# The last stage of a decode block: its result in two PSUM banks, the last weight row in two column halves, and one load for w_up

## The chip, the cores and the metric

The kernel runs on one core of one Trainium2 chip. The metric is the device time in microseconds of one execution, given as the median of several runs. A profiled execution also has a span, from the first to the last instruction that the profiler recorded; the execution's time is a little longer than its span.

## What is computed

One token (`x`, 1024 numbers) goes through attention with a long key/value cache and then through a gated feed-forward block, both with a layer norm ahead and the input added behind. All inputs and the output are bfloat16.

```python
h  = x + softmax(q @ K^T * Dh**-0.5) @ V @ wo        # 32 query heads, 4 KV heads, 65536 keys, Dh = 128
n  = layernorm(h)
h2 = h + (gelu(n @ w_gate) * (n @ w_up)) @ w_down    # 1024 -> 3584 -> 1024
```

The caches hold 134 MB, and wq, wo, w_gate, w_up and w_down together 39 MB. Every byte of them is read once. The result is 1024 numbers.

## The kernel before, in words

**The stream.** All big inputs come through one ring of three slots in SBUF, 64 KB per partition each. `load` (L172) takes the next slot when its offset is 0, or an offset inside the present slot, and issues one DMA from SyncE. The order of the loads in the program is the order in which they are issued and queue up: wq, then the K and V caches in pieces of 8 MB, then wo (one load, L479), w_gate (one load, L535), w_up (two loads of four chunks each, L539 to L542) and w_down (five loads of 14, 7, 4, 2 and 1 rows, L560 and L579). A load is issued as soon as what lay at its place in the slot has been read.

**The weights of the last stages.** Each weight matrix has its contraction index spread over 128 partitions, and the rest of that index gives "chunks" or "rows": 32 for wo, 8 for w_gate and w_up, 28 for w_down. One row of w_down is 128 x 1024 bfloat16, 256 KB, of which each partition holds 2 KB. The vector to be multiplied is the stationary operand, padded to 32 columns with zeros (`padded`, L235), and the weights stream past it. A stationary operand of 32 columns fills a quarter of TensorE, so four matmuls with different column groups (`tile_position=(0, 32*g)`) can run beside each other; their results stand in partitions 0, 32, 64 and 96 (and the 31 below each hold what belongs to the zeros).

**TensorE's helper.** `mm` (L153) issues one matmul. With `loaded=True` the matmul is issued without a weight load of its own (L158), and uses what the one before it in the same column group loaded; the trace puts matmuls with a weight load at L156 and those without at L158. `keep` (L135) ties each TensorE instruction behind the one before it in the program, so TensorE's order is the program's.

**wo.** `row_mm` (L469) gives each row of wo to one column group, in two halves of 512 columns, the second with `loaded`. `evac` (L247) copies the two banks to `at_r`, one on VectorE, one on ScalarE.

**The residual.** `f_ps` (L486) is one PSUM bank tile of 128 x 256 float32. `out_mm` (L488) issues four matmuls of 256 columns, one for each column group g, which covers the output's columns 256g to 256g+255. L494 adds up `at_r` over partitions with a stationary operand of ones (float32, two passes for each matmul), L496 adds x. What stands in `f_ps` now is h. L498 turns it to columns for the second layer norm. `f_ps` is not emptied: the rows of w_down are added to it later.

**Gate and up.** `up_mm` (L528) issues seven matmuls of 512 columns for a chunk, 56 for a matrix, into two banks. `turned` (L507) copies the two banks to SBUF (VectorE and ScalarE) and transposes them with eight float32 transposes on TensorE. For w_gate VectorE and ScalarE then form the gelu; for w_up VectorE multiplies (L557) and writes `act_bf`, which L238 pads to `actz`, the stationary operand for w_down.

**w_down.** For each of the five loads, L583 issues one `out_mm` for each row: four weight loads and four matmuls of 256 columns. Behind `turned` and behind the first two loads `keep_busy` (L572) issues 8, 8 and 5 matmuls of 128 x 512 into a bank that nobody reads (`w_ps`).

**The end.** `seen_by_sync` (L565) makes SyncE wait for the last eight loads, for the last ScalarE copy and for GpSimd. L587 casts `f_ps` (97 partitions x 256) to `o_fin` in bfloat16 on VectorE, and L588 writes it out from partitions 0, 32, 64 and 96, four runs of 512 bytes.

Of the kernel before, what the change touches and what calls it, by code (L numbers as in the profile page):

```python
# [12 lines left out]
F32 = mybir.dt.float32  # L13
# [4 lines left out]
def kernel(  # L18
# [13 lines left out]
    nc = tc.nc  # L32
    P = 128
    D = A_x.shape[-1]
# [4 lines left out]
    F = B_w_gate.shape[1]  # L39
    DC = D // P  # L40
    FC = F // P
# [5 lines left out]
    CW = 16384  # L47
# [20 lines left out]
    ones_f = low.tile([P, P], F32, name="ones_f")  # L68
# [8 lines left out]
    x_row = lead.tile([P, D // 4], BF16, name="x_row")  # L77
    ident_bf = lead.tile([P, P], BF16, name="ident_bf")
# [5 lines left out]
    o_fin = lead.tile([P, D // 4], BF16, name="o_fin")  # L84
# [10 lines left out]
    ps_m = ctx.enter_context(tc.tile_pool(name="ps_m", bufs=1, space=PSUM))  # L95
# [48 lines left out]
    def pe(op):  # L144
        return keep(op, "pe")
# [7 lines left out]
    def mm(out, lhsT, rhs, start, stop, loaded=False, tile_position=None, skip_group_check=False):  # L153
        t = nc.tensor
        if not loaded:
            return pe(t.matmul(out, lhsT=lhsT, rhs=rhs, start=start, stop=stop, tile_position=tile_position,  # L156
                               skip_group_check=skip_group_check))
        op = t.add_instruction(mybir.InstMatmult(  # L158
            name=nc.get_next_instruction_name(), engine=t.engine, start_tensor_calc=start, stop_tensor_calc=stop,
            tile_size=(lhsT.shape[0], lhsT.shape[1]), tile_position=tile_position or (0, 0), ldweights=False,  # L160
            bass_skip_group_check=skip_group_check,
            ins=[t.lower_ap(rhs), t.lower_ap(lhsT, for_matmul_weights=True)], outs=[t.lower_ap(out, opt=True)]))
        reuses.add(op.ins.name)
        return pe(op)
# [5 lines left out]
    loads, pools, last = [], [], {}  # L170

    def load(src, off=0):  # L172
        n, w = src.shape[1], src.shape[2]
        if off == 0:
            slot[0] = (slot[0] + 1) % NSLOT
        assert off + n * w <= 2 * CW
        o = slot[0] * 2 * CW + off
        tv = ring[:, o:o + n * w].rearrange("p (n w) -> p n w", w=w)
        loads.append(nc.sync.dma_start(out=tv, in_=src).ins)
        return tv  # L180
# [20 lines left out]
    for bp in range(4):  # L201
        s0 = 64 * (bp // 2) + bp % 2
        nc.vector.tensor_copy(out=esel[:, bp, :, :],
                              in_=ident_bf[:, s0:s0 + 63:2].unsqueeze(1).to_broadcast([P, 4, 32]))
# [30 lines left out]
    def padded(i, vec, ncols, name):  # L235
        t = pt_tile(i, [P, ncols, 32], BF16, name)
        pools.append(nc.gpsimd.memset(t[:], 0.0))
        nc.vector.tensor_copy(out=t[:, :, 0], in_=vec)  # L238
        return t
# [171 lines left out]
    for n, u in enumerate(units):  # L411
        what, g, li = u
# [53 lines left out]
    def row_bank(name):  # L466
        return ps_w.tile([P, 512], F32, name=name, tag="w")
# [11 lines left out]
    wv = load(wo_v[:])  # L479
    for c in range(Hq):  # L480
        row_mm(at_ps, o2z[:, c, :], wv[:, c, :], c, c < 4, c + 4 >= Hq)
    at_r = low.tile([P, DS, 512], F32, name="at_r", tag="sc0")
    for s in range(DS):
        evac(at_r[:, s, :], at_ps[s][:], s)
    OW = D // 4
    f_ps = ps_f.tile([P, OW], F32, name="f_ps")  # L486

    def out_mm(stat, mov, first, last, groups=range(4)):  # L488
        for g in groups:
            mm(f_ps[32 * g:32 * g + 32, :], stat, mov(g), first, last, tile_position=(0, 32 * g),  # L490
               skip_group_check=True)
# [8 lines left out]
    layernorm_cols(h_t[:, :, 0], hn_bf[:], "ln2")  # L500
    hnz = padded(2, hn_bf[:], DC, "hnz")

    assert F <= CW and FC == 28
    GB = CW // F
    NF = FC // 4

    def turned(banks, name, tag):  # L507
        outs = []
        both = low.tile([P, 2, 512], F32, name=name + "_ev", tag=tag)
        for k in range(2):  # L510
            ng = min(4, NF - 4 * k)
            ev = both[:, k, :]
            last["act"] = evac(ev[0:32 * ng, :], banks[k][0:32 * ng, :], k)
            t_ps = ps_t.tile([P, 4, P], F32, name=name + "_t", tag="T")
            for b in range(4):
                tr(t_ps[:, b, 0:32 * ng], ev[0:32 * ng, b::4], ident_f[0:32 * ng, 0:32 * ng])
            outs.append((16 * k, 4 * ng, t_ps[:, :, 0:32 * ng:32]))
        return outs
# [5 lines left out]
    u_banks = [row_bank("wu_ps") for _ in range(2)]  # L524
    gv = B_w_gate.rearrange("(p c) n -> p c n", c=DC)
    uv = B_w_up.rearrange("(p c) n -> p c n", c=DC)

    def up_mm(banks, w, c, loaded):  # L528
        for s in range(NF):
            g = s % 4  # L530
            mm(banks[s // 4][32 * g:32 * g + 32, :], hnz[:, c, :],
               w.rearrange("p (m j) -> p m j", j=FC)[:, :, 4 * s:4 * s + 4],
               c == 0, c == DC - 1, loaded=(loaded or s >= 4), tile_position=(0, 32 * g))
# [2 lines left out]
    for c in range(DC):  # L536
        up_mm(g_banks, wg[:, c, :], c, False)
    g_t = turned(g_banks, "wg", "sc1")
    for c0 in range(0, DC, GB):  # L539
        wu = load(uv[:, c0:c0 + GB, :], c0 * F)  # L540
        for cc in range(GB):
            up_mm(u_banks, wu[:, cc, :], c0 + cc, False)  # L542
    g_ap = top.tile([P, FC], F32, name="g_ap")
    for j0, nj, src in g_t:
        nc.vector.tensor_copy(out=by_j(g_ap, j0, nj), in_=src)
# [11 lines left out]
        nc.vector.tensor_tensor(out=by_j(act_bf, j0, nj), in0=src, in1=by_j(gl, j0, nj), op=ALU.mult)  # L557

    wd_v = B_w_down.rearrange("(p c) n -> p c n", p=P)
    sizes = [14, 7, 4, 2, 1]  # L560
    assert sum(sizes) == FC
    actz = padded(3, act_bf[:], FC, "actz")
    w_ps = row_bank("w_ps")

    def seen_by_sync(ins):  # L565
        seen = nc.sync.nop()
        for i in ins:
            tc.add_manual_dep(seen.ins, i.name,
                              mybir.DependencyInfo(mybir.DependencyClass.Sync, mybir.DependencyReason.DATA),
                              reason="seen")  # L570

    def keep_busy(n, src):  # L572
        for _ in range(n):
            mm(w_ps[:], ident_bf[:], src, True, True)

    keep_busy(8, wu[:, 0, 0:512])
    busy = [8, 5, 0, 0, 0]
    c0 = 0
    for sz, nb in zip(sizes, busy):  # L579
        wv = load(wd_v[:, c0:c0 + sz, :], c0 * D)  # L580
        for cc in range(sz):
            c = c0 + cc
            out_mm(actz[:, c, :], lambda g: wv[:, cc, g * OW:(g + 1) * OW], False, c + 1 == FC)  # L583
        c0 += sz
        keep_busy(nb, wv[:, 0, 0:512])
    seen_by_sync(loads[-8:] + [last["act"].ins] + [x.ins for x in pools])
    nc.vector.tensor_copy(out=o_fin[0:97, :], in_=f_ps[0:97, :])  # L587
    nc.sync.dma_start(out=out[0, 0].rearrange("(g n) -> g n", n=OW), in_=o_fin[0:97:32, :])  # L588


# [28 lines left out]
```

## Time and profile before

| what | value |
|---|---|
| median of 3 runs | 408.0 us (407.77 to 408.11) |
| the profiled execution's own time | 407.74 us |
| its span | 405.9 us |
| mean granted TensorE clock | 0.899 |
| busy: TensorE, VectorE, ScalarE, GpSimd | 72%, 50%, 10%, 2% of the span |
| read from HBM | 173.02 MB, 426 GB/s over the span |

Between the profiled execution's time and its span lie 1.84 us that the profile doesn't cover. The page cuts the span into 40 equal slices and gives each engine's busy share in tenths. The chain of waits goes back from the last instruction: at each step to what released it, or to the instruction ahead of it on its engine. The timeline lists instructions in order of time, merged by kind: start, how long the merged group took, engine, line, operation, output and input, the count, and in brackets the idle time before it and what ended it. PE is TensorE's matmuls, PEld its weight loads, DVE VectorE, ACT ScalarE, POOL GpSimd, SP SyncE. A first matmul that waited for a DMA starts when that load has landed, so these starts tell when the pieces of the stream arrive.

### The profile page before, as it was taken

To read this page: it belongs to the slowest core of one execution; us is meant where nothing else is said; L and a number is where in the kernel's file an instruction comes from. 1 tells how busy PE (TensorE), PEld (TensorE's weight loads), DVE (VectorE), ACT (ScalarE), POOL (GpSimd) and SP (SyncE) were. 2 spreads that over 40 slices of the span, in tenths; PEclk is the share of its full clock that TensorE was granted. 3 is DMA by queue.
4 is the path that set the end of the run, shared out by engine and by line. 5 is a ranking of instruction groups with operands and counts; after the bars stand their busy time and mean duration, and the time that the engine had idled before them with its cause. 6 is when DMAs were issued, how large, how long until landed. Compare 5 with 4: busy or idle time off the path is not lost.

```text
span 405.9 us, 2664 instructions
## 1 busy us (share of the span) xinstructions
PE 294.3 (72%) x1500; PEld 64.2 (16%) x750; DVE 202.4 (50%) x185; ACT 40.9 (10%) x63; POOL 7.5 (2%) x17
## 2 busy tenths in 40 slices
PE   0170677758899695979969957997695999636285
PEld 0110111111111110221111113111110211212042
DVE  0200989999829744971595387609943000220110
ACT  1001000023000031100000312000031000100000
POOL 2000000000000000000000000000010000000000
PEclk9997689987899999769999967899999699886889
DMA  9999999999999999999999999999999999999995
GB/s 413 413 413 439 491 408 413 420 440 478 420 408 426 446 465 420 408 433 452 452 420 415 433 452 446 421 421 433 446 446 420 428 433 452 405 443 407 432 423 234
DMA packets 3773, 173.19 MB, mean 427 GB/s; under 512 B 425, under 2 KB 433, under 8 KB 689
## 3 DMA queue, kind: packets, MB, share of 16 engines
q1 hardware_dynamic: 3752, 173.02, 98.7%
q8 instruction: 9, 0.15, 0.1%
q14 instruction: 4, 0.02, 0.0%
q10 hardware_dynamic: 8, 0.00, 0.0%
HBM read 173.02 MB, written 0.00 MB: 426 GB/s over the span
## 4 chain that ended last, share of the span: by engine, by line
DMA 41%; PE 35%; DVE 21%; ACT 2%; issue 1%; SPq 0%; ACTq 0%; DVEq 0%
DMA ring<-in_A_k_cache_dram 30%; DVE ring L289 16%; PE acc_ps L158 16%; DMA ring<-in_B_w_down_dram 11%; PE qk_ps L156 6%; PE acc_ps L156 5%; PE qk_ps L158 5%; DVE mx L314 2%; ACT sc L310 2%; DVE pT L347 1%; PE o_ps L156 1%; PE at_ps L156 1%; DVE acc_sb L370 1%; PE at_ps L158 1%; PE nb_ps L156 0%
## 5 line engine op out<-in xcount | busy, mean ns | idle before, releaser
L289 DVE STREAM_TRANSPOSE ring<-ring 128x2048 uint32<-128x2048 uint32 x64 | 142.7, 2279 | 35.5 <-DMA ring<-in_A_k_cache_dram 35.5
L156 PE MATMUL qk_ps<-ring,wsel 128*128 128x512 bf16 x256 | 107.2, 419 | 49.1 <-DVE ring L289 30.0
L158 PE MATMUL qk_ps<-ring,wsel 128*128 128x512 bf16 x256 | 106.4, 416 | 0.0
L158 PE MATMUL acc_ps<-ring,pT 128*128 128x512 bf16 x384 | 105.1, 383 | 0.0
L156 PEld LDWEIGHTS <-wsel 128*128 128x128 bf16 x256 | 27.0, 105 | 156.0 <-issue 139.1
L156 PE MATMUL acc_ps<-ring,pT 128*128 128x512 bf16 x128 | 49.2, 384 | 0.0
L314 DVE TENSOR_REDUCE mx<-qk_ps 128x1 f32<-128x1024 f32 x16 | 19.5, 1220 | 24.6 <-ACT sc L310 18.6
L347 DVE STREAM_TRANSPOSE pT<-pT 128x1024 bf16<-128x1024 bf16 x16 | 19.3, 1227 | 23.8 <-ACT pT L341 23.8
L156 PEld LDWEIGHTS <-pT 128*128 128x128 bf16 x128 | 12.8, 100 | 90.7 <-issue 90.7
L310 ACT COPY sc<-qk_ps 128x1024 f32<-128x1024 f32 x12 | 12.1, 1012 | 148.2 <-PE qk_ps L158 148.2
L370 DVE COPY acc_sb<-acc_ps 32x512 f32<-32x512 f32 x8 | 5.3, 666 | 29.4 <-PE acc_ps L158 29.4
L341 ACT ACTIVATE pT<-sc,nbias 128x1024 bf16<-128x1024 f32 x12 | 13.7, 1142 | 44.9 <-DVE nbias L333 41.9
L156 PE MATMUL ln_tot<-ln_s,ones_f 128*128 128x1 f32 x8 | 1.9, 311 | 13.4 <-DVE ln_s L210 11.6
L156 PE MATMUL q_ps<-ring,xnz 128*32 128x512 bf16 x32 | 5.0, 598 | 9.1 <-DMA ring<-in_A_wq_dram 9.1
L156 PE MATMUL o_ps<-sel,acc_sb 128*128 128x8 f32 x32 | 6.6, 335 | 5.8 <-DVE rl L384 5.4
L372 ACT COPY acc_sb<-acc_ps 32x512 f32<-32x512 f32 x8 | 4.6, 577 | 58.6 <-DVE acc_sb L370 58.6
L156 PE MATMUL wu_ps<-ring,hnz 128*32 128x512 bf16 x32 | 4.7, 502 | 7.7 <-DMA ring<-in_B_w_up_dram 7.7
L156 PE MATMUL wg_ps<-ring,hnz 128*32 128x512 bf16 x32 | 4.8, 539 | 7.1 <-DMA ring<-in_B_w_gate_dram 7.1
L248 DVE COPY q_ev<-q_ps 128x512 f32<-128x512 f32 x1 | 0.7, 692 | 14.0 <-PE q_ps L158 14.0
L341 ACT ACTIVATE pT<-qk_ps,nbias 128x1024 bf16<-128x1024 f32 x4 | 4.5, 1113 | 29.8 <-PE acc_ps L158 16.8
L156 PEld LDWEIGHTS o_ps<-sel,acc_sb 128*128 128x128 f32 x32 | 6.3, 293 | 6.1 <-issue 5.1
L156 PEld LDWEIGHTS <-hnz 128*32 128x32 bf16 x64 | 3.2, 115 | 20.8 <-issue 17.3
(105 smaller groups left out, 89.1 us busy)
## 6 DMA issues: line engine op xcount, KB each, us to landing
ring<-in_B_w_gate_dram SPq DMA_DIRECT2D x1, 7168.0 KB
ring<-in_B_w_up_dram SPq DMA_DIRECT2D x2, 3584.0 KB, 37.6
ring<-in_B_w_down_dram SPq DMA_DIRECT2D x1, 3584.0 KB, 38.2
ring<-in_B_w_down_dram SPq DMA_DIRECT2D x1, 1792.0 KB, 41.6
ring<-in_B_w_down_dram SPq DMA_DIRECT2D x1, 1024.0 KB, 43.3
ring<-in_B_w_down_dram SPq DMA_DIRECT2D x1, 512.0 KB
ring<-in_B_w_down_dram SPq DMA_DIRECT2D x1, 256.0 KB, 44.2
ring<-in_A_k_cache_dram SPq DMA_DIRECT2D x8, 39.4
```

The lines of the kernel that those rows point to most:

```text
L156: return pe(t.matmul(out, lhsT=lhsT, rhs=rhs, start=start, stop=stop, tile_position=tile_position, skip_group_check=skip_group_check))
L158: op = t.add_instruction(mybir.InstMatmult(name=nc.get_next_instruction_name(), engine=t.engine, start_tensor_calc=start, stop_tensor_calc ...
L248: return nc.vector.tensor_copy(out=dst, in_=src) if k % 2 == 0 else nc.scalar.copy(out=dst, in_=src)
L289: dv(nc.vector.transpose(out=kt[:, c * w:(c + 1) * w], in_=kt[:, c * w:(c + 1) * w]))
L310: ac(nc.scalar.copy(out=sc[:], in_=flat))
L314: dv(nc.vector.tensor_reduce(out=state[("mx", g)][:, li:li + 1], in_=flat, axis=AX.X, op=ALU.max))
L341: ac(nc.scalar.activation(out=flat, in_=state.pop(("sc", g, li)), func=ACT.Exp, bias=st["nbias"][:, 0:1], scale=scale, accum_out=st["lpart ...
L347: dv(nc.vector.transpose(out=flat, in_=flat))
L370: dv(nc.vector.tensor_copy(out=acc_sb[sl, :], in_=acc[sl, c, :]))
L372: ac(nc.scalar.copy(out=acc_sb[sl, :], in_=acc[sl, c, :]))
```

## The change

- w_up comes in one load, and its 56 matmuls follow that load.
- The result of the last stage stands in two PSUM banks: `f_ps[:, 0:128]` for the output's columns 0 to 511, and a new tile `fb_ps` of 128 x 128 for columns 512 to 1023. In each, column group g covers 128 columns. `half_mm` issues one matmul of 128 columns.
- h is formed a second time, in this layout, by eight float32 matmuls over `at_r` and eight with x; they stand behind the transposes of w_up in TensorE's order. The first h, in `f_ps`, still feeds the layer norm.
- w_down comes in loads of 16, 8 and 3 rows, and the 28th row in two loads of 512 columns. A row of the first 27 is four weight loads and eight matmuls of 128 columns; the second of each two reuses the weights. A half of the last row is four weight loads and four matmuls.
- `keep_busy` issues 4 matmuls behind the seeds of h, 10 behind the 16 rows and 3 behind the 8 rows.
- The first half is cast by VectorE, the second by ScalarE, each 97 x 128, and one DMA writes both: eight runs of 256 bytes.

```diff
-    assert F <= CW and FC == 28
-    GB = CW // F
+    assert DC * F <= 2 * CW and FC == 28
...
-    for c0 in range(0, DC, GB):
-        wu = load(uv[:, c0:c0 + GB, :], c0 * F)
-        for cc in range(GB):
-            up_mm(u_banks, wu[:, cc, :], c0 + cc, False)
+    wu = load(uv[:])
+    for c in range(DC):
+        up_mm(u_banks, wu[:, c, :], c, False)
...
-    sizes = [14, 7, 4, 2, 1]
-    assert sum(sizes) == FC
...
-    keep_busy(8, wu[:, 0, 0:512])
-    busy = [8, 5, 0, 0, 0]
+    HW = D // 2
+    QW = HW // 4
+    fb_ps = ps_m.tile([P, QW], F32, name="fb_ps", tag="misc")
+    halves = [f_ps[:, 0:QW], fb_ps[:]]
+
+    def half_mm(b, g, stat, mov, first, last, loaded=False):
+        mm(halves[b][32 * g:32 * g + 32, :], stat, mov, first, last, loaded=loaded, tile_position=(0, 32 * g),
+           skip_group_check=True)
+
+    for g in range(4):
+        for b in range(2):
+            half_mm(b, g, ones_f[:, 0:32], at_r[:, b, g * QW:(g + 1) * QW], True, False)
+    for g in range(4):
+        for b in range(2):
+            q = 2 * b + g // 2
+            half_mm(b, g, ident_bf[:, 32 * q:32 * q + 32], x_row[:, g % 2 * QW:(g % 2 + 1) * QW], False, False)
+
+    def down_rows(wv, c0, n, bs):
+        for cc in range(n):
+            c = c0 + cc
+            for g in range(4):
+                for b in bs:
+                    o = (b if len(bs) > 1 else 0) * HW + g * QW
+                    half_mm(b, g, actz[:, c, :], wv[:, cc, o:o + QW], False, c + 1 == FC, loaded=(b > bs[0]))
+
+    keep_busy(4, wu[:, 0, 0:512])
     c0 = 0
-    for sz, nb in zip(sizes, busy):
+    for sz, nb in zip([16, 8, 3], [10, 3, 0]):
         wv = load(wd_v[:, c0:c0 + sz, :], c0 * D)
-        for cc in range(sz):
-            c = c0 + cc
-            out_mm(actz[:, c, :], lambda g: wv[:, cc, g * OW:(g + 1) * OW], False, c + 1 == FC)
+        down_rows(wv, c0, sz, [0, 1])
         c0 += sz
         keep_busy(nb, wv[:, 0, 0:512])
-    seen_by_sync(loads[-8:] + [last["act"].ins] + [x.ins for x in pools])
-    nc.vector.tensor_copy(out=o_fin[0:97, :], in_=f_ps[0:97, :])
-    nc.sync.dma_start(out=out[0, 0].rearrange("(g n) -> g n", n=OW), in_=o_fin[0:97:32, :])
+    assert c0 == FC - 1
+    o_b = o_fin[:].rearrange("p (b j) -> p b j", b=2)
+    for b, put in ((0, nc.vector.tensor_copy), (1, nc.scalar.copy)):
+        wv = load(wd_v[:, c0:FC, b * HW:(b + 1) * HW], c0 * D + b * HW)
+        down_rows(wv, c0, 1, [b])
+        if b == 1:
+            seen_by_sync(loads[-8:] + [last["act"].ins] + [x.ins for x in pools])
+        put(out=o_b[0:97, b, :], in_=halves[b][0:97, :])
+    nc.sync.dma_start(out=out[0, 0].rearrange("(b g n) -> g b n", b=2, g=4),
+                      in_=o_b[0:97:32, :, :])
```

## Prediction, made before the result was known

> **What bounds the kernel now.** First the page: its head, the slices, the chain.
>
> ```profile
> span 405.9 us, 2664 instructions
> ...
> DMA  9999999999999999999999999999999999999995
> ...
> HBM read 173.02 MB, written 0.00 MB: 426 GB/s over the span
> ...
> DMA 41%; PE 35%; DVE 21%; ACT 2%; issue 1%; SPq 0%; ACTq 0%; DVEq 0%
> ```
>
> The DMA engines are full in 39 of 40 slices, and no byte is read twice. So the time is the stream's length, about 402.65 us, and a tail behind its last byte. The chain of waits over the last 36 us shows the tail:
>
> ```profile
> 358.49 44.16 DMA ring<-in_B_w_down_dram
> 402.65 0.04 issue
> 402.69 0.32 PE f_ps L156 x4
> 403.00 0.02 issue
> 403.03 0.42 DVE o_fin L587
> ```
>
> Behind the last w_down row come one row of matmuls, the cast and the write. Last the timeline, where each f_ps group starts when a load has landed, and SyncE's write closes the work:
>
> ```profile
> 394.10 1.71 PE L156 MATMUL f_ps<-ring,actz 128*32 128x256 bf16 x56 [1.58 <-DMA ring<-in_B_w_down_dram]
> ...
> 398.42 0.95 PE L156 MATMUL f_ps<-ring,actz 128*32 128x256 bf16 x28 [0.77 <-DMA ring<-in_B_w_down_dram]
> ...
> 400.86 0.62 PE L156 MATMUL f_ps<-ring,actz 128*32 128x256 bf16 x16 [0.31 <-DMA ring<-in_B_w_down_dram]
> ...
> 402.06 0.40 PE L156 MATMUL f_ps<-ring,actz 128*32 128x256 bf16 x8 [0.58 <-DMA ring<-in_B_w_down_dram]
> ...
> 402.69 0.29 PE L156 MATMUL f_ps<-ring,actz 128*32 128x256 bf16 x4 [0.23 <-DMA ring<-in_B_w_down_dram]
> ...
> 403.48 0.64 SPq L588 DMA_DIRECT2D out_dram<-o_fin  x1
> ```
>
> TensorE waits for all five loads, so the stream and not TensorE sets 402.69. From there the tail is 0.34 to the cast, 0.45 to the write, 2.42 from the write to the span's end. About 0.2% of the time, 0.8 us, is what a measurement here can tell from no change, and the edit can shorten only the first two terms, 0.79 us together.
>
> **The stream, part by part.** Landings go by those starts: 7 rows in 4.32 us, 4 in 2.44, 2 in 1.20, 1 in 0.63, so 0.61 to 0.63 us a row. The new pieces should land at 394.10 + 2 x 0.617 = 395.33 (16 rows), 400.86 - 0.61 = 400.25 (24), 402.06 (27), about 402.37 (first half), 402.69 (second). Shorter runs could cost: the single row took 0.02 us more than its share of the two rows ahead (0.63 against 0.60, rounding and all), so two halves may cost 0 to 0.05. One load less for w_up could save as much. I take zero for both.
>
> w_up's single load needs its whole slot free. Its second half was issued at 347.19 (SyncE's queue in the timeline), 21 us ahead of w_gate's landing at 368.72; one load issued then still queues behind w_gate. The w_down loads stand behind it on SyncE, issued from 355.88; they need wo's rows read (done by 357.6), which doesn't move. Nothing stalls; cover 21 us.
>
> **TensorE before w_down.** All 56 w_up matmuls now wait for 385.62. w_gate is the row for that: one load, 56 matmuls from 368.72, VectorE's copy of the first bank at 374.08, 5.36 later, half of it at the low clock (the stage 385.6 to 389.3 had a granted clock of 0.50 too). So the copy for w_up starts at 390.98 instead of 388.84, 2.14 us late, and all up to `actz` with it: ready at 391.30 + 2.14 = 393.44, while TensorE leaves the transposes at 390.85 + 2.14 = 392.99. The seeds of h have as many columns as L494 and L496 had, which took 358.45 to 359.19 at the low clock: 0.37 to 0.74 us. Four `keep_busy` matmuls at 0.215 (seven recorded took 1.67, one 0.379) are 0.86. TensorE is free at 394.3 to 394.6; the 16 rows land at 395.33. Cover 0.7 us: price nothing.
>
> **TensorE in w_down.** A row of 256-column matmuls costs 0.109 us now: 56 starts span 1.71 - 0.27 over 13 row steps. A row becomes eight matmuls of 128 columns, as many columns, with four weight loads as before. That pairs in one column group don't block the other groups is shown by wo, where each group got two matmuls in a row, the second at L158: four of 512 columns went every 0.215 us (starts at 355.67, 355.89, 356.10). By columns a new row costs 0.11. But issuing may bind: the shortest matmuls of the trace tell.
>
> ```profile
> 351.82 0.25 PE L156 MATMUL o_ps<-o_sb,osel 32*128 32x32 bf16 x4 [0.30 <-DVE o_sb L455]
> ```
>
> Each takes 171 ns by its row, so starts are (0.25 - 0.171)/3 = 26 ns apart, where a quarter of a 128-column matmul's columns flow. Eight at 26 would be 0.21 us a row. These four were in no column groups, so the price lies between 0.11 and 0.21; I take 0.11, the row with the same tiling.
>
> With r for a row: 16 r from 395.33, ten `keep_busy` 2.46 (2.15, and 0.3 for the change of tiling ahead of them; today 0.16 passes from the end of the 14 rows' record at 395.81 to the next start at 395.97), 8 r, three 0.85, 3 r and the halves r. By r = 0.11, the 16 rows and ten matmuls end at 399.6, before 400.25; 8 rows and three end at 402.0, just before 402.06; 3 rows at 402.4; the halves meet their landings. If TensorE never waits again, it starts the last matmul at 395.33 + 2.46 + 0.85 + 28 r - 0.03 = 398.61 + 28 r, past 402.69 once r exceeds 0.146; from 400.25 the second stretch gives a like bound, 0.135.
>
> The Trainium skill ("TensorE: Matmul & The Clock Gate", on the 56 ns gap) says that start-to-start never falls below about 25 ns however short the matmul; the 26 ns agree. It speaks against the edit, which halves matmuls: by it a row is 0.20 and the forecast about 409.3. "TensorEngine Tiling (Array Packing)", Key Properties, says that tiles operate independently; if the floor holds for each tile alone, a row stays 0.11. No row here has short matmuls in column groups.
>
> **The tail.** The last piece is one half: four 128-column matmuls. Their record interpolates between 171 ns (32 columns) and 273 (256) to 215, 0.06 less, so the second copy starts 0.28 after the landing. The copy is ScalarE's:
>
> ```profile
> L270 ACT CAST wsel<-qr_ps 32x128 bf16<-32x128 f32 x4 | 1.0, 256 | 1.8 <-PE qr_ps L156 1.7
> ```
>
> That is the same form, 128 float32 of PSUM to bfloat16, and takes 0.256 against the 0.424 of VectorE's cast, 0.17 less. VectorE's half is beside it: landed 402.37, matmuls to 402.65, cast 0.29 (from 0.424 at 256 columns and 0.692 at 512), done 402.94, while ScalarE ends at 403.23. ScalarE's queue holds nothing else then. Sum: 0.06 + 0.17 = 0.23 off the tail; SyncE writes at 403.26. SyncE also waits for one engine more; its waits pass while the copies run. The write has eight runs of 256 bytes for four of 512. Below nothing I see no reason; above, x's load, four runs too, kept its queue 1.08 us against 0.64 here, so +0.44 for the issue, and if the 1.0 us that SyncE waits for the landing doubled, +1.0. The five w_down loads have 128 runs each and took 3.04 us of issuing, 0.61 apiece, no more than the four runs: I take 0.
>
> "DMA: Bandwidth & Descriptors", Specifications, calls 512 bytes the least for line rate, and says smaller ones are read, modified and written. It gives no price for eight of them, and no run here shows one.
>
> **The sum.** 405.9 - 0.23 = 405.7 in span; with the 1.84 outside it, 407.5 for the profiled execution, which had 407.74. That one lay 0.26 under the median of 408.0, so the forecast is 408.0 - 0.2 = 407.8, a gain too small to tell.
>
> **Rivals.**
> - *A tie or a little slower, 408.3 (18%).* TensorE takes 13.7 ns for each instruction, as today (eight in 0.109 us): twelve make r = 0.164, the last start 403.20, 0.51 late, less 0.23: +0.3. Or the write costs more, up to +1.0 - 0.2. For it: more instructions for the same columns. Against: those eight are explained by columns alone.
> - *TensorE becomes the bound, 409.5 (13%).* r = 0.21 puts the last start at 404.5, 1.8 late; less 0.23 is +1.5. It decides from r = 0.154, where 0.23 of lateness eats the gain. For it: the 26 ns. Against: wo's four groups side by side.
> - *The clock is late, 407.8 to 408.3.* If w_up ran wholly at the low clock, `actz` would come some 1.5 us later and the waits of 0.65 us ahead of the 8 rows and the 0.7 ahead of the 16 take most of it up. It is counted in the other cases.
> - *The change doesn't shorten the tail, 408.0:* the cast wasn't last, or the second bank brings nothing. The chain shows the cast on the path, so this is within the first case.
>
> **How the numbers follow.** 62% for the forecast (shortest matmul record 171, w_up's load saving 0.05, and the runs' own spread of 0.2 reach down to 407.4; upward to 408.0), 18% for the tie, up to 408.8, 13% for TensorE, 3% for something else slower, 4% for a gain over 0.8 us that I can't derive. Range 407.4 to 408.8 holds 80%. Faster by over 0.2% 0.04, within 0.80, slower 0.16.
>
> **What would show it.** f_ps and fb_ps groups starting at about 395.3, 400.25, 402.1, 402.4 and 402.7 with "DMA w_down" as the end of their idle time; 27 rows at 0.11 us; ScalarE's cast near 0.26, starting 0.28 after the last landing; SyncE's write near 403.26 and 2.4 us from it to the end. It is wrong if the last groups have no idle time ahead of them (TensorE bound), if the last landing moves from 402.7, or if the write takes longer.

## The result and the profile after

The changed kernel takes 408.82 us (median of 14 runs, 408.61 to 409.06), the kernel before 408.0 (14 runs, 407.7 to 408.39): 1.0021 times as long (1.0014 to 1.0028). The forecast was 407.8, so the sign was wrong, and the time lies just past the range. The page of the changed kernel:

```profile
span 406.9 us, 2822 instructions
...
PE 294.8 (72%) x1634; PEld 64.1 (16%) x774; DVE 202.1 (50%) x185; ACT 41.2 (10%) x64; POOL 7.5 (2%) x17
...
q8 instruction: 9, 0.15, 0.1%
...
HBM read 173.02 MB, written 0.00 MB: 425 GB/s over the span
```

The same lines of the page of the kernel before:

```profile
PE 294.3 (72%) x1500; PEld 64.2 (16%) x750; DVE 202.4 (50%) x185; ACT 40.9 (10%) x63; POOL 7.5 (2%) x17
...
q8 instruction: 9, 0.15, 0.1%
```

The bytes are the same, the span is 1.0 us longer. TensorE has 1634 + 774 = 2408 recorded instructions, before it had 1500 + 750 = 2250. The lines of q8 will matter below. The timeline of the changed kernel's last 12 us, cut to each first group behind a landing, the last group of the 16 rows (397.37) and the tail:

```profile
395.64 0.24 PE L156 MATMUL f_ps<-ring,actz 128*32 128x128 bf16 x4 [1.16 <-DMA ring<-in_B_w_down_dram]
...
397.37 0.25 PE L158 MATMUL fb_ps<-ring,actz 128*32 128x128 bf16 x4
...
400.48 0.24 PE L156 MATMUL f_ps<-ring,actz 128*32 128x128 bf16 x4 [0.60 <-DMA ring<-in_B_w_down_dram]
...
403.21 0.24 PE L156 MATMUL f_ps<-ring,actz 128*32 128x128 bf16 x4 [0.90 <-DMA ring<-in_B_w_down_dram]
...
403.81 0.24 PE L156 MATMUL fb_ps<-ring,actz 128*32 128x128 bf16 x4
...
403.83 0.29 DVE L611 CAST o_fin<-f_ps 97x128 bf16<-97x128 f32 x1 [10.52 <-PE f_ps L156]
404.10 0.27 ACT L611 CAST o_fin<-fb_ps 97x128 bf16<-97x128 f32 x1 [12.45 <-PE fb_ps L156]
404.39 0.68 SPq L612 DMA_DIRECT2D out_dram<-o_fin  x1
```

TensorE is never late: at the landings of 16, 24 and 27 rows it had been idle for 0.6 to 1.2 us, and the last half's matmuls (403.81) start 0.27 behind the first half's, where the step from group to group is 0.06. The tail did what it should: from the last half's first matmul (403.81) to the write (404.39) pass 0.58 us, where there were 0.79. The write to the end takes 406.9 - 404.39 = 2.51 instead of 2.42. But the loads are late. 16 rows came at 395.64 and 24 at 400.48, 0.2 to 0.3 behind the forecast; the three rows came at 403.21 instead of 402.06, and the last half at 403.81, 1.12 behind the last row of before. The sum, 1.12 - 0.21 + 0.09 = 1.00, is the span's difference.

At the 24 rows the landing is 0.23 behind the forecast, at the 27 rows 1.15: most of the loss arises in the stream's last three microseconds. The DMA view from 402 to 404 us, in slices of 0.05 us, first before and then after (each packet is counted where it starts):

```profile
GB/s 164 164 246 41 451 41 0 0 0 0 0 0 0 0 0 0 0 0 0 0 0 0 0 0 0 0 0 0 0 0 0 0 0 0 0 0 0 0 0 0
```

```profile
GB/s 184 144 123 123 225 102 41 21 41 143 20 0 0 0 41 20 20 20 20 41 21 20 20 20 20 20 41 0 0 0 0 0 0 0 0 0 0 0 0 0
```

Before, the last weights start by 402.3 and are in by 402.38. After, most is in by 402.55, and then something trickles at 20 to 41 GB/s until 403.35. Sixteen engines together move 426, some 27 each: this is about what one engine moves, about 1 us behind the others. The same view from 396 to 402 us has, besides the stream's queue q1, before and after:

```profile
q1 hardware_dynamic: 451, 2.23, 89.2%
```

```profile
q1 hardware_dynamic: 445, 2.17, 87.5%
q8 instruction: 1, 0.02, 1.0%
```

One packet of a queue that the page calls "instruction" is in that stretch after, and none before. By the trace's packets it has 16 KB and lasts from 400.36 to 401.30. Both kernels have nine of them. Before, the ninth starts at 402.243, six thousandths of a microsecond behind a completion packet of the stream at 402.237 (behind the data of each load the trace has 16 packets of 4 bytes; they are called completion packets here).

**Theories.** *R, refill:* these packets bring TensorE's instructions, 16 KB at a time, over the DMA engines that carry the stream. Each costs the DMA engine that carries it more than a microsecond. The change gives TensorE more instructions, so the ninth comes 2 us earlier and in front of weights instead of behind them. *S, size of runs:* the loads of 6 KB, 1 KB and 1 KB runs are slow. *U:* the one load of w_up makes the stream late.

### The profile page after: what moved, and what is told of

The parts are those of the page before. It is cut to its first block, busy times and chain, and to the rows that moved or that the text cites. A ratio compares the mean times of both kernels' runs of the same rounds, so it can differ in the third digit from the quotient of the medians.

```text
span 406.9 us, 2822 instructions
## 1 busy us (share of the span) xinstructions
PE 294.8 (72%) x1634; PEld 64.1 (16%) x774; DVE 202.1 (50%) x185; ACT 41.2 (10%) x64; POOL 7.5 (2%) x17
## 4 chain that ended last, share of the span: by engine, by line
DMA 40%; PE 38%; DVE 17%; ACT 2%; issue 1%; ACTq 0%; DVEq 0%
DMA ring<-in_A_k_cache_dram 30%; PE acc_ps L158 16%; DVE ring L289 12%; DMA ring<-in_B_w_down_dram 11%; PE qk_ps L156 8%; PE qk_ps L158 7%; PE acc_ps L156 5%; DVE mx L314 2%; ACT sc L310 2%; DVE pT L347 1%; PE o_ps L156 1%; DVE acc_sb L370 1%; PE at_ps L156 1%; PE at_ps L158 1%; ACT acc_sb L372 1%
## 5 line engine op out<-in xcount | busy, mean ns | idle before, releaser
L156 PE MATMUL qk_ps<-ring,wsel 128*128 128x512 bf16 x256 | 108.8, 425 | 49.4 <-DVE ring L289 30.2
L158 PE MATMUL qk_ps<-ring,wsel 128*128 128x512 bf16 x256 | 108.3, 423 | 0.0
```

The source lines that it names most:

```text
L158: op = t.add_instruction(mybir.InstMatmult(name=nc.get_next_instruction_name(), engine=t.engine, start_tensor_calc=start, stop_tensor_calc ...
```

## The experiments

Each time is a median; the kernel before ran beside each (medians 407.92 to 407.96).

**1. Before, with 48 tiny matmuls ahead.** Only TensorE's instruction count changes.

```diff
+    fill_ps = ps_m.tile([P, 32], F32, name="fill_ps", tag="misc")
+    for _ in range(48):
+        mm(fill_ps[:], ident_bf[:], ident_bf[:, 0:32], True, True)
     assert D // 4 == 32 * DC
```

> Theory R (refill): TensorE's instructions come in pieces of 16 KB over the DMA engines that carry the stream; each costs the engine that brings it some 1.4 us; before needs eight inside the stream and the ninth starts at 402.24, behind its engine's last weight, while the changed kernel, with more TensorE instructions, gets the ninth at 400.36, in front of weights. By R the kernel before with 48 tiny matmuls (96 instructions with their weight loads) ahead of everything, in time that TensorE waits for w_q, becomes slower by 1.0 to 1.4 us: 409.0 to 409.4. Theory S (size of runs): the shorter runs of the last loads make the stream late. By S this kernel, whose loads are those of before, stays at 408.0.

Measured: 409.02 (6 runs, 408.85 to 409.54), ratio 1.0027 (1.0015 to 1.0039). Its timeline, where the 48 matmuls stand at the start, and the last two loads:

```profile
1.51 1.46 PE L156 MATMUL fill_ps<-ident_bf 128*128 128x32 bf16 x48 [1.51 <-POOL ident_bf masks.py:199]
```

```profile
403.34 0.40 PE L156 MATMUL f_ps<-ring,actz 128*32 128x256 bf16 x8 [0.62 <-DMA ring<-in_B_w_down_dram]
403.93 0.29 PE L156 MATMUL f_ps<-ring,actz 128*32 128x256 bf16 x4 [0.19 <-DMA ring<-in_B_w_down_dram]
```

1.46 us of work in the first 3 us, while TensorE waits for wq anyway, make the last row land 1.24 us later (403.93 for 402.69), with loads that are those of before. All nine q8 packets moved, from 55.3, 115.8, 164.0 ... 390.1, 402.2 to 28.6, 96.0, 144.4 ... 374.0, 398.4: they follow TensorE's instructions. This is R; by S and by U nothing would have moved.

**2. The changed kernel with fewer TensorE instructions.** Rows of wo and chunks of w_gate and w_up are left out.

```diff
-    for c in range(Hq):
-        row_mm(at_ps, o2z[:, c, :], wv[:, c, :], c, c < 4, c + 4 >= Hq)
+    for c in range(8):
+        row_mm(at_ps, o2z[:, c, :], wv[:, c, :], c, c < 4, c + 4 >= 8)
...
-    for c in range(DC):
+    for c in (0, DC - 1):
         up_mm(g_banks, wg[:, c, :], c, False)
...
-    for c in range(DC):
+    for c in (0, DC - 1):
         up_mm(u_banks, wu[:, c, :], c, False)
```

> The changed kernel with fewer TensorE instructions: 24 of wo's 32 rows, six of w_gate's eight and six of w_up's eight chunks are loaded but left out of the sums (the output is not the reference's). Its loads are those of the changed kernel. By R the ninth refill falls behind the stream, the last half lands near 402.7 and the time is 407.6 to 407.9, faster than before by the 0.2 us of the tail. By S it stays at 408.8.

Measured: 408.33, but spread from 407.69 to 409.43 (10 runs). It doesn't decide. A stage of the profiled execution, which took 409.35 (start and end, length, then busy time of each engine, then the granted clock, here 0.50), shows why for that execution:

```profile
394.00:399.00 5.00, 3.43 (x128) 2.84 (x63) 0.00 (x0) 0.00 (x0) 0.00 (x0) 0.50 0.92 395
```

In this stage the clock was 0.50; ten `keep_busy` matmuls took 3.20 us, the eight rows waited for them until 402.24, and the casts began at 404.64. What fell was the cover that the forecast had counted on, by a cause of the experiment's own. Three of the ten runs, at 407.69 to 407.86, are where R put them. The profiled execution's weights were all in by 402.52, although a refill, here the eighth, stood in the stream at 400.26, almost where the changed kernel's ninth did: a refill in front of the last weights doesn't cost by itself (the last section comes back to this).

**3. Before, with w_up in one load.**

```diff
-    for c0 in range(0, DC, GB):
-        wu = load(uv[:, c0:c0 + GB, :], c0 * F)
-        for cc in range(GB):
-            up_mm(u_banks, wu[:, cc, :], c0 + cc, False)
+    wu = load(uv[:])
+    for c in range(DC):
+        up_mm(u_banks, wu[:, c, :], c, False)
```

> The kernel before with w_up in one load, and nothing else of the change. TensorE's instructions are as many as before. By R: 408.0, within 0.2. A third theory, U (one load of w_up makes the stream or actz late, since w_up's matmuls started 0.35 us later in the changed kernel's trace), gives 408.3 to 408.8.

Measured: 407.97 (10 runs), ratio 1.0 (0.9991 to 1.0009). U falls. Its w_up landed at 386.00, as late as in the changed kernel (385.98, before 385.62); over all runs here that first start lies between 385.5 and 386.5, so the 0.3 us there is not the change's. What sets it was not tried.

**4. The changed kernel with its last row in one load.**

```diff
+    wv = load(wd_v[:, c0:FC, :], c0 * D)
+    down_rows(wv, c0, 1, [0, 1])
     for b, put in ((0, nc.vector.tensor_copy), (1, nc.scalar.copy)):
-        wv = load(wd_v[:, c0:FC, b * HW:(b + 1) * HW], c0 * D + b * HW)
-        down_rows(wv, c0, 1, [b])
```

> The changed kernel with its 28th row in one load of 2 KB runs, then both halves' matmuls and both casts side by side. TensorE's instructions differ from the changed kernel's by four. By R the refill still falls into the stream: 408.8 to 409.0. By S, if the 1 KB runs are what is slow, it falls back to 408.0 to 408.2.

Measured: 409.03 (6 runs), ratio 1.0028 (1.0015 to 1.0041). The timeline still has the three rows late, and the ninth refill is at 400.06:

```profile
403.09 0.24 PE L156 MATMUL f_ps<-ring,actz 128*32 128x128 bf16 x4 [1.16 <-DMA ring<-in_B_w_down_dram]
```

The 1 KB runs are not what is slow. The 6 KB runs of the three rows were not undone by themselves; run 8 below keeps them and has them on time.

**5. The first 16 rows folded.** A kernel with the same result, the changed kernel's loads, casts and write, and TensorE instructions as few as before (1536 + 712 = 2248).

```diff
-    c0 = 0
-    for sz, nb in zip([16, 8, 3], [10, 3, 0]):
+    dn_ps = [row_bank("dn_ps") for _ in range(2)]
+    wv = load(wd_v[:, 0:16, :])
+    for c in range(16):
+        row_mm(dn_ps, actz[:, c, :], wv[:, c, :], c, c < 4, c + 4 >= 16)
+    s_r = low.tile([P, 2, 512], F32, name="s_r", tag="sc1")
+    for b in range(2):
+        nc.vector.tensor_tensor(out=s_r[:, b, :], in0=dn_ps[b][:], in1=at_r[:, b, :], op=ALU.add)
+    keep_busy(10, wv[:, 0, 0:512])
+    for b in range(2):
+        for g in range(4):
+            half_mm(b, g, ones_f[:, 0:32], s_r[:, b, g * QW:(g + 1) * QW], False, False)
+    c0 = 16
+    for sz, nb in zip([8, 3], [3, 0]):
```

The seeds over `at_r` go, those with x open the banks, and in `keep_busy` all but the first matmul of a burst get `loaded=True`.

> The changed kernel with fewer TensorE instructions and the same result: the first 16 rows go the way of wo's rows (each row to one column group, one weight load and two matmuls of 512 columns, three instructions instead of twelve), VectorE adds their two banks to at_r, and the ones matmuls fold the sum into the two halves; keep_busy loads its weights once a burst. Loads, casts and write are the changed kernel's. By R the ninth refill falls behind the stream as in the kernel before, and what is left is the shorter tail: 407.6 to 407.9, 0.2 faster than before. By S 408.8 stays.

Measured: 407.98 (11 runs, 407.55 to 409.32), ratio 1.0001 (0.9992 to 1.001). In the profiled execution the refill is gone from the stream (403.7); 0.8 of the loss is gone from the median, but the gain isn't there. Two stages of the profiled execution, the slowest of the runs:

```profile
393.40:395.90 2.50, 0.81 (x3) 0.09 (x1) 0.18 (x1) 0.00 (x0) 0.00 (x0) 1.00 0.96 413
395.90:399.30 3.40, 3.36 (x32) 0.67 (x15) 0.00 (x0) 0.00 (x0) 0.00 (x0) 0.50 1.02 434
```

TensorE worked 0.81 of 2.5 us, and the clock fell to 0.50 for the next 3.4: the 32 matmuls took all of them, and the last half waited for TensorE. That is one execution; the others' clocks in this stage aren't known.

**6. Fewer instructions again, w_up whole.** As in 2, without the third edit.

> The run with fewer instructions again, now with w_up whole: only 24 of wo's rows and six of w_gate's chunks are left out of the sums (the output is not the reference's). In the last one the clock was low in the w_down stage and TensorE late; with w_up's 56 matmuls in place the clock should be full from w_up on. By R: no refill between 393 and 402, last half at 402.7 to 402.9, 407.6 to 407.9. By S: 408.8.

Measured: 407.73, eight of ten runs from 407.49 to 407.81, the two others 408.52 and 409.04; ratio 0.9998 (0.9989 to 1.0007). Where the changed kernel's fourteen runs never came below 408.61, the same loads with fewer TensorE instructions come to 407.7. S falls. The profiled execution is the one of 408.52; its stream lost 0.7 us long before, around 60 to 77 us, where runs of 64 KB took 2.55 us for 2.42, so its late landings tell nothing of the change. The expectation "no refill between 393 and 402" was wrong: the eighth came at 399.70, on an engine that was ahead (below).

**7. Before, with 8 tiny matmuls.** As in 1, with `range(8)`.

> The kernel before with 8 tiny matmuls (16 instructions) ahead instead of 48. By R the ninth refill is asked for 16 instructions earlier; how near the kernel before stands to the edge isn't known: if the 16 bring it in front of some of the last weights, 408.3 to 409.2, if not 408.0. By S 408.0.

Measured: four runs at 408.00 to 408.06 and four at 409.09 to 409.87; ratio of all 1.0018 (1.0006 to 1.003). The profiled execution is one of the longer four, and its timeline shows the edge:

```profile
402.08 0.40 PE L156 MATMUL f_ps<-ring,actz 128*32 128x256 bf16 x8 [0.60 <-DMA ring<-in_B_w_down_dram]
...
404.21 0.29 PE L156 MATMUL f_ps<-ring,actz 128*32 128x256 bf16 x4 [1.73 <-DMA ring<-in_B_w_down_dram]
```

All weights are in by 402.38, as before. But the refill starts at 402.169, in front of one engine's 4-byte completion packet, which goes out at 403.103 where the other engines sent theirs by 402.37. The last row "lands" 1.5 us late though its bytes are there. The packet's delay is 0.7 of that; from its end to the matmul pass 1.1 us where 0.3 passed before, and no view says why. So the kernel before stands some 16 instructions from the edge.

**8. Folded, with more work for the clock.** Run 5 with `keep_busy` 9, 6, 3 instead of 4, 10, 3.

> The run that folds the first 16 rows, with keep_busy at 9, 6 and 3 matmuls instead of 4, 10 and 3. In its profile the clock had fallen to half from 395.9 to 399.3, after 1.65 us without TensorE work, and the last halves waited for TensorE; its other executions went down to 407.55. By R with the clock kept full: 407.6 to 407.8 in most executions, 0.2 to 0.3 faster than before. If the folding itself (VectorE's two additions, 1.3 us) is what is late, it stays near 408.0.

Measured: 407.84 (11 runs, 407.6 to 408.46), before beside it 407.96; ratio 1.0 (0.9991 to 1.0008). The timeline of the profiled execution (407.7) is the forecast's tail nearly to the number:

```profile
402.76 0.29 DVE L619 CAST o_fin<-f_ps 97x128 bf16<-97x128 f32 x1 [3.52 <-PE f_ps L156]
402.79 0.24 PE L156 MATMUL fb_ps<-ring,actz 128*32 128x128 bf16 x4
402.79 0.10 PEld L156 LDWEIGHTS <-actz 128*32 128x32 bf16 x3 [0.23 <-issue]
403.07 0.27 ACT L619 CAST o_fin<-fb_ps 97x128 bf16<-97x128 f32 x1 [10.48 <-PE fb_ps L156]
403.37 0.68 SPq L620 DMA_DIRECT2D out_dram<-o_fin  x1
```

Last landing 402.79, write 0.58 behind it; the refill comes at 403.11, behind everything. Against the changed kernel about 1.0 us is back. Against the kernel before no difference can be told in time: 0.1 in the medians, within the interval. The spans say more: their median is 405.9 here and 406.2 for the 21 executions of the kernel before beside it, which is about the 0.2 of the shorter tail. But 5 of the 11 executions have 2.1 to 2.5 us outside their span, where none of the 21 has over 1.92.

**9. The same with the last row in one load.** The edit of run 4 on run 8.

> The same with the 28th row in one load of 2 KB runs and its two halves cast side by side, VectorE and ScalarE. It tells what the two column halves are worth beside the two casts: if only the cast counts, the same within 0.1; if the half row's fewer matmuls behind the last landing count, 0.06 to 0.1 slower than with two loads.

Measured: 407.93 (11 runs), ratio 0.9996 (0.9987 to 1.0005). The medians of 8 and 9 differ by 0.09 the way that was expected for the half row, the ratios the other way: inconclusive. Two of run 9's eleven executions, too, have 2.24 us outside their span. One is the profiled one, whose ninth refill starts at 407.08, past the span's end at 405.9. That a refill behind the end makes the execution longer would fit, but wasn't tried.

## Why the prediction was wrong

- **What bounds the kernel: right.** The stream and the tail behind it still set the time.
- **TensorE ahead of w_down: right.** w_up's copy came at 390.86 (forecast 390.98), the seeds and four `keep_busy` ended at 394.5, and the 16 rows found TensorE idle.
- **A row at 0.11 us: right.** The 16 rows' groups start from 395.64 to 397.37, 31 steps of four matmuls: 0.056 each, 0.112 a row (the row of before, 0.109 in the prediction, is 0.111 by its own division, 1.44 over 13). So short matmuls in four column groups start 14 ns apart on average. The 26 ns of the four matmuls at 351.82 don't carry over to them. The Trainium skill's 25 ns ("TensorE: Matmul & The Clock Gate", on the 56 ns gap), by which a row was estimated at 0.20, doesn't hold across column groups in these runs; "TensorEngine Tiling (Array Packing)", Key Properties, with its independent tiles, agrees.
- **The tail: right.** 0.21 less, forecast 0.23; ScalarE's cast 0.27, forecast 0.256. From the write to the end it took 0.09 more in these two traces, forecast 0, well inside the bounds.
- **The stream's landings: wrong, and this is the step that failed.** "I take zero for both" priced the loads by their runs alone, and "past 402.69 once r exceeds 0.146" priced TensorE's added instructions by TensorE's time alone. The instructions themselves come over the same sixteen DMA engines. The page of before had the line, nine packets on the instruction queue, and the text itself counted twelve instructions a row for eight. The term that is missing is the ninth refill in front of the last weights. The last landing came 1.12 us late, as the three rows did already (1.15). In run 8, with the same loads and the refill behind them, it came at 402.79, so the refill is 1.02 of the 1.12; where the other 0.10 comes from wasn't measured. Run 1 brought the loss about with nothing but instructions; runs 5, 6 and 8 took it away with the changed loads in place.
- **The rivals.** The slower cases put the loss on TensorE's time or the write. 408.82 lies between their numbers, but neither mechanism is what happened.
- **The chances.** 16% for slower by over 0.2% were the 13% for TensorE as the bound and 3% for a cost outside the listed ones; the tie's 18% reached up to 408.8 and lay within 0.2%. What happened is in the 3%.

The Trainium skill knows the mechanism: "Runtime: NRT & Kernel Launch", Instruction fetch mechanics, has instructions refilled in blocks of 16 KiB, 256 instructions, by DMA. The runs agree: 16 KB a packet, and 239 to 286 recorded TensorE instructions, 260 on average, between the starts of two in the kernel before. The section calls the cost of a boundary mostly hidden; here the ninth one costs 1.1 us (run 1, 409.02 for 407.92).

What stays open: which of TensorE's instructions asks for a refill, and how long the request waits, was not measured. Why w_up's landing moves by up to 1 us between runs isn't known either.

## What to carry to other kernels

When DMA bounds a kernel to its end, count the instructions of the busiest engine as DMA traffic: the instruction queue's line in the profile says how many refills there are, and the packet's time says whether one stands in front of the last bytes. That alone doesn't cost: in runs 2 and 6 one at 400.26 and 399.70 brought no such delay. What counted, by the sorting of packets in the next section, was a second refill on one engine. An edit that adds instructions anywhere, even in idle time at the start, can shift a refill into the tail; one that saves some can shift it out. Before work that only covers waits is trimmed, look at the granted clock of the stage that follows.

## What the runs showed of the hardware

- **A refill costs its engine about 1.4 us, not only the 0.9 that its own packet takes.** In the kernel before the one at 390.06 took 0.93, and the run behind it 1.57 instead of 1.06. In the changed kernel the one at 400.36 took 0.93, and the next runs 0.65 and 0.31 instead of 0.23.
- **Refills go round the engines, and the most refilled engine sets the end.** An engine's packets follow each other end to start, and each engine has the same order of sizes, so they can be sorted to engines (an inference). In the kernel before, the six refills up to 321 us fell on six engines, which ended their 64 KB runs at 351.05 to 351.43, while eight of the others ended theirs at 349.65 to 350.00. So a refill on an engine that is ahead costs nothing, as the eighth in run 6. The ninth fell on the engine of the first in runs 1 and 4, which was already behind. In run 1 seven of the eight engines without a refill were done at 400.6 to 401.2, the seven with one at 402.0 to 402.4, and the one with two at 403.5; in run 4 the one with two was done at 403.3, the seven with one by 402.2.
- **A refill can hold back a completion alone.** In run 7 the weights were in by 402.38, and one engine's 4-byte packet went out at 403.10, 0.7 us behind the last of the others.
- **The clock can be at half behind a wait of 1.65 us, and needn't behind one of 1.58.** In run 5's profiled execution the granted clock was 0.50 from 395.9 to 399.3, behind 1.65 us without TensorE work, and then TensorE, not the stream, set the end. In the kernel before TensorE waited 1.58 us up to 394.10, and the clock stayed at 1.00 up to 399.3. What decides between the two wasn't tried.
